# Attention with a gated MLP on one core: the score shift split on another engine, another order at the start and at the end

## The chip, the cores and the metric

The kernel runs on one core of a Trainium2 chip. A core has five engines that run their own queues side by side: TensorE (PE) multiplies matrices, VectorE (DVE) and ScalarE (ACT) work elementwise and can read the accumulator memory (PSUM), GpSimd (POOL) works elementwise on the on-chip memory (SBUF) alone, and SyncE (SP) issues the transfers between SBUF and device memory. Each queue is worked off in order, and engines wait for each other by semaphores. The metric is the device time of one execution in microseconds (us), as the median of several runs.

## What is computed

The sequence has 2048 tokens of 512 numbers, with 32 heads of 16 and 1792 hidden columns in the MLP. All inputs are fp32.

```python
xn = layernorm(x)                               # eps 1e-5, no scale or offset
q, k, v = split(xn @ wqkv)                      # 32 heads of 16
p = softmax(q @ k.T * 16 ** -0.5)               # 2048 x 2048 in each head
s = concat(p @ v) @ wo
h = relu(xn @ w1 + b1) ** 2
g = silu(h @ w2 + b2)
out = x + s * g
```

## The kernel before

**Split numbers.** A product of fp32 accuracy is made of three faster ones. A tensor is split into a high part (rounded to fp32r, the format of the faster product) and a low part (what the rounding left), and `a @ b` becomes high x high, high x low and low x high, summed in PSUM. The helper `split` (line 95) makes both parts on GpSimd: a `tensor_scalar` (times 1, plus 0) for the high part, a `tensor_tensor` subtraction for the low one.

**The head.** Sixteen token tiles of 128 rows are loaded, normalized, transposed on TensorE and split. `ln_stats` takes mean and variance on VectorE and the square root on ScalarE; `ln_norm` makes the two scalars of each token on VectorE and the normalized tile on ScalarE (line 1236); `ln_high` transposes it on TensorE (four products with the identity) and copies the high part out of PSUM on ScalarE; `ln_low` takes the low part on VectorE. `split_w` splits the weights of the first q and k columns, high part on ScalarE, low part on GpSimd. The loop at line 1322 hands these out for tile after tile, and `pump(n)` puts n products of q, k or v in between. The order of PE's queue there is that of the program. The first products belong to the k columns (m = 4) of the first 256 tokens, thus to tiles 0 and 1; `qk_terms` puts them in an order by the parts that they need.

**The lead and the loop.** A unit is one group of four heads and 512 queries; there are 32. For each, 64 products of raw scores (64x512, line 320) are made ahead, each reduced to its maximum per row on VectorE (line 327). `shift(u)` turns the maxima of unit u by a 32x32 transpose (`tr`), negates and splits them into `sh` with two VectorE instructions (lines 373 and 376), and SyncE stores `sh` in device memory (`keep`) and loads it back as two more rows of the q tile (`back`, four transfers). The K tile has rows of 1.0 at the same place (`fill_ring("ka", ...)`), so that the second product of the scores (line 1281) comes out with the maximum taken off; ScalarE takes its exponential (line 1293), and line 408 multiplies it with v. The code counts by slots: in each the two halves of PE's rows work on different products, among them the MLP and later the output product, and in a slot eight PV products (line 408, four heads by one block of keys) stand together. In the first chunk of the MLP GpSimd also splits w1 and w2, which it later reads back from device memory or keeps. In the loop, the order on ScalarE, VectorE, GpSimd and SyncE is that of the program.

**The end.** `unit_final` closes the last unit for the last four token tiles: twelve products add the last heads to four sums in PSUM (`out(tt, n)`; n = 2 needs the low part that GpSimd makes), `gate` multiplies each by g on VectorE, tile 1 gets its residual sum by a product with the identity and a ScalarE copy, and `add` adds it for tiles 0 and 2 on GpSimd and for tile 3 on VectorE. Four stores end the kernel.

Of the kernel before, what the change touches and what calls it, by code (L numbers as in the profile page):

```python
# [9 lines left out]
F32 = mybir.dt.float32  # L10
F32R = mybir.dt.float32r
AF = mybir.ActivationFunctionType
ALU = mybir.AluOpType
# [4 lines left out]
P = 128  # L18
# [7 lines left out]
NT = S // P  # L26
NQ = H // 4
NU = NQ * 4
# [29 lines left out]
def kernel(  # L58
# [11 lines left out]
    nc = tc.nc  # L70
# [44 lines left out]
    with ExitStack() as ph:  # L115
# [253 lines left out]
        def shift(u):  # L369
            tr = sp.tile([P, 32], F32, name="tr", bufs=1)  # L370
            nc.vector.transpose(tr, mxs[u])
            sh = sp.tile([P, 2, 32], F32R, name="sh", bufs=1)
            nc.vector.scalar_tensor_tensor(
                sh[:, 0], tr, -2.0, tr, op0=ALU.mult, op1=ALU.add
            )
            nc.vector.scalar_tensor_tensor(
                sh[:, 1], tr, -1.0, sh[:, 0].bitcast(F32),
                op0=ALU.mult, op1=ALU.subtract,
            )

            def keep():
                nc.sync.dma_start(
                    sh_d[u].rearrange("b c i n -> (b c) i n"), sh.bitcast(F32)
                )
# [536 lines left out]
        def unit_final(po):  # L921
# [24 lines left out]
                g = parts[tt][0]  # L946
                nc.vector.tensor_tensor(g, pss[tt], g, op=ALU.mult)

            def add(tt, eng):
                g, s = parts[tt]  # L950
                eng.tensor_tensor(g, g, s, op=ALU.add)

            def store(tt, queue):
                queue.dma_start(of[1536 + tt * P : 1536 + (tt + 1) * P, :], parts[tt][0])

            for i in range(2):
                for tt, n in ((0, 0), (0, 1), (1, 0), (1, 1), (0, 2), (1, 2)):
                    out(2 * i + tt, n)
            for tt in range(4):
                gate(tt)  # L960
            nc.tensor.matmul(both, ident, parts[1][0], start=False, stop=True)
            nc.scalar.activation(parts[1][0], both, AF.Copy)
            add(0, nc.gpsimd)
            add(2, nc.gpsimd)
            add(3, nc.vector)
            store(0, nc.sync)
            store(1, nc.scalar)
            store(2, nc.scalar)
            store(3, nc.sync)

        ph.enter_context(tc.manual_schedule(engines={mybir.EngineType.PE}))
        qs = ExitStack()
# [57 lines left out]


# [179 lines left out]
        xts = {}  # L1211
# [17 lines left out]
        def ln_norm(t):  # L1229
            rstd = rstds.pop(t)  # L1230
            xn = xp.tile([P, D], F32, name="xn", bufs=3)
            nc.vector.reciprocal(rstd[:, 0:1], rstd[:, 0:1])
            nc.vector.tensor_scalar(
                rstd[:, 1:2], mvs.pop(t)[:, 0:1], rstd[:, 0:1], -1.0, op0=ALU.mult, op1=ALU.mult
            )
            nc.scalar.activation(xn, xts[t], AF.Identity, bias=rstd[:, 1:2], scale=rstd[:, 0:1])
            xts[t] = xn

        def ln_high(t):
# [78 lines left out]
            load_x(t)  # L1318
        for vt in vts:
            nc.vector.memset(vt[:, :, DH:], 1.0)  # L1320
        fill_ring("ka", 0, 1.0)
        for i in range(NT + 3):
            if i in (2, 3):

                kos = slice(2 * i - 4, 2 * i - 2)
                if i == 2:
                    ln_norm(1)
                    ln_high(0)
                    split_w(wa_t, kos, slice(0, 2 * P), raw_m[:, kos])
                else:  # L1330
                    ln_low(0)
                    ln_high(1)
                    split_w(wa_t, kos, slice(0, 2 * P), raw_m[:, kos])
                    ln_norm(2)
                ln_stats(i)
            else:
                if i < NT:
                    ln_stats(i)
                if 0 <= i - 1 < NT:
                    ln_norm(i - 1)  # L1340
                if 0 <= i - 3 < NT:
                    ln_low(i - 3)
                if i == 4:

                    pump(4)
                if 0 <= i - 2 < NT:
                    ln_high(i - 2)
            if 5 <= i < 9:
                split_w(wa_t, i - 5, slice(2 * P, 2 * P + D), raw_v[:, i - 5], True)
            let_go()  # L1350
            if 9 <= i < 11:
                fill_ring("ka", 1, 1.0, (32 + 64 * (i - 9),))
            if i in (11, 12):
                fill_ring("qm", i - 11, 0.0)
            if i == 11:
# [40 lines left out]
        fill_ring("qm", 2, 0.0)  # L1396
        for n in range(4):
            fill_ring("qe", n, 0.0)
        fill_ring("ka", 2, 1.0)
        pump(47)  # L1400
        led.append(0)
        at = order.index(("v", 2, 0)) + 1
# [323 lines left out]
```

## Time and profile before

| | |
|---|---|
| median of 3 runs | 1624.79 us (1623.78 to 1625.50) |
| the profiled execution | 1623.51 us, its span 1621.7 us |
| PE busy | 1608.4 us (99%) |
| VectorE busy | 1362.7 us (84%) |
| ScalarE busy | 1189.5 us (73%) |
| GpSimd busy | 520.7 us (32%) |
| 16 DMA engines, mean of packets' time in the main queue | 44.3% of the span |
| VectorE: maxima from PSUM (line 327, main group) | 1910 x 682 ns |
| VectorE: transposes of the shift (line 371) | 32 x 200 ns |

A row of the timeline reads: start (us from the span's start), duration, engine, line, operation, written tile, read tiles, shapes, count of merged instructions, and in brackets the idle time ahead and what ended it. A row of the windows view gives the stretch, its length, the busy time and count of PE, PE's weight loads, VectorE, ScalarE and GpSimd, then the granted clock of TensorE, the share of the DMA engines and GB/s. The chain of waits goes back from the last instruction to what released each step.

### The profile page before, as it was taken

The numbers are of one execution on the slowest core, as the hardware profiler recorded it, in microseconds if no ns is written. First come the engines' busy times: TensorE is split into PE (matmuls) and PEld (weight loads), VectorE is DVE, ScalarE is ACT, GpSimd is POOL, SyncE is SP. The second block draws the span as 40 slices with busy tenths as digits, with TensorE's granted clock in tenths as the row PEclk, the third lists the DMA queues.
The fourth block names the chain that finished last, engine by engine and source line by source line (L and its number), as shares of the span: only waits on it lengthen the run. The fifth ranks groups of instructions, "written<-read, shape, count | busy, mean of one in ns | idle before, by whom it ended". The sixth has DMA issues, their size and how long they took to land.

```text
span 1621.7 us, 36039 instructions
## 1 busy us (share of the span) xinstructions
PE 1608.4 (99%) x13660; PEld 933.3 (58%) x13660; DVE 1362.7 (84%) x2364; ACT 1189.5 (73%) x2349; POOL 520.7 (32%) x550
## 2 busy tenths in 40 slices
PE   8999999999999999999999999999999999999998
PEld 6898665556546654664466446645654565445543
DVE  6486888888888888888888888888888888887755
ACT  7212677777777777877777777777777777778886
POOL 6436667133113311331132113311331123214621
PEclk9999999999999999999999999999999999999999
DMA  8876556434342333423333334323432262236654
GB/s 295 239 237 230 175 165 154 132 94 130 79 105 89 110 84 91 132 87 101 91 108 99 88 92 118 113 73 90 131 109 71 65 162 76 65 106 219 213 176 169
DMA packets 164028, 209.18 MB, mean 129 GB/s; under 512 B 59120, under 2 KB 79088, under 8 KB 162288
## 3 DMA queue, kind: packets, MB, share of 16 engines
q1 hardware_dynamic: 163568, 206.37, 44.3%
q8 instruction: 108, 1.77, 0.5%
q14 instruction: 64, 0.52, 0.1%
q10 hardware_dynamic: 288, 0.52, 0.1%
HBM read 148.90 MB, written 56.34 MB: 127 GB/s over the span
## 4 chain that ended last, share of the span: by engine, by line
PE 98%; DVE 1%; DMA 0%; SPq 0%; issue 0%; DVEq 0%
PE po L408 31%; PE pd_t L258 19%; PE pm_t L320 17%; PE se L1281 15%; PE pd_t L226 5%; PE pm_t L1157 4%; PE pm_t L226 2%; PE pd_t L1157 1%; PE se L1127 1%; PE se L1061 1%; PE se L320 1%; DVE mx L327 0%; PE pm_t L1243 0%; PE pd_t L1127 0%; DMA xt<-in_A_x_dram 0%; PE po L1061 0%
## 5 line engine op out<-in xcount | busy, mean ns | idle before, releaser
L327 DVE TENSOR_REDUCE mx<-pm_t 128x1 f32<-128x512 f32 x1910 | 1187.0, 682 | 163.1 <-PE pm_t L320 80.2
L1293 ACT ACTIVATE pt<-se 128x512 f32<-128x512 f32 x1894 | 976.1, 613 | 235.0 <-PE se L1281 192.5
L320 PE MATMUL pm_t<-ka,qm 64*128 64x512 f32 x1910 | 761.7, 419 | 0.1
L1281 PE MATMUL se<-qe,ka 64*128 64x512 f32 x2005 | 677.6, 396 | 0.0
L408 PE MATMUL po<-pt,v 128*32 128x512 f32 x3820 | 520.8, 605 | 0.2 <-DVE tsm L851 0.2
L320 PEld LDWEIGHTS pm_t<-ka,qm 64*128 64x128 f32 x1910 | 335.1, 184 | 236.5 <-DVE mx L327 225.5
L1281 PEld LDWEIGHTS se<-qe,ka 64*128 64x128 f32 x2005 | 339.1, 184 | 19.7 <-ACT xr L1293 1.7
L258 PEld LDWEIGHTS pd_t<-xc,w1s 64*128 64x128 f32 x2352 | 292.0, 186 | 82.2 <-issue 82.2
L258 PE MATMUL pd_t<-xc,w1s 64*128 64x256 f32 x2352 | 332.2, 288 | 0.0
L258 PE MATMUL pd_t<-w2t,hT 64*128 64x512 f32 x1080 | 300.5, 410 | 0.0
L258 PEld LDWEIGHTS pd_t<-w2t,hT 64*128 64x128 f32 x1080 | 179.1, 184 | 82.3 <-issue 75.5
L573 POOL TENSOR_TENSOR r<-r 128x512 f32<-128x512 f32 x56 | 58.2, 1040 | 370.5 <-ACT r L570 370.5
L408 PEld LDWEIGHTS po<-pt,v 128*32 128x32 f32 x3820 | 76.7, 108 | 147.2 <-issue 125.8
L592 POOL TENSOR_TENSOR u<-u,b_t 128x512 f32<-128x512 f32 x16 | 20.6, 1288 | 317.7 <-ACT u L591 283.9
L327 DVE TENSOR_REDUCE mx<-se 128x1 f32<-128x512 f32 x121 | 77.9, 685 | 26.1 <-PE se L320 21.6
L457 POOL TENSOR_TENSOR ot<-ot,hl 128x512 f32<-128x512 f32 x27 | 34.7, 1286 | 168.5 <-DMA hl<-r_d 101.6
L570 ACT ACTIVATE r<-pd_t,b_t 128x256 f32<-128x256 f32 x112 | 46.9, 470 | 57.0 <-PE pd_t L258 55.9
L1157 PE MATMUL pm_t<-xT,wr_t 64*128 64x512 f32 x408 | 73.8, 388 | 0.0
L100 POOL TENSOR_TENSOR hT<-r,hT 128x512 fp32r<-128x512 f32 x56 | 72.2, 1290 | 4.7
L226 PE MATMUL pd_t<-w2t,hT 64*128 64x512 f32 x264 | 68.9, 393 | 0.0
L1157 PEld LDWEIGHTS pm_t<-xT,wr_t 64*128 64x128 f32 x408 | 58.2, 185 | 4.4
L226 PEld LDWEIGHTS pd_t<-w2t,hT 64*128 64x128 f32 x264 | 47.1, 184 | 6.4 <-issue 0.2
(174 smaller groups left out, 1352.2 us busy)
## 6 DMA issues: line engine op xcount, KB each, us to landing
w1s<-w_d SPq DMA_DIRECT2D x196, 256.0 KB
qm<-q_d SPq DMA_DIRECT2D x384, 32.0 KB
ka<-k_d SPq DMA_DIRECT2D x96, 128.0 KB
qe<-q_d SPq DMA_DIRECT2D x384, 32.0 KB
q_d<-hl SPq DMA_DIRECT2D x16, 512.0 KB
g<-g_d SPq DMA_DIRECT2D x32, 256.0 KB
k_d<-hl SPq DMA_DIRECT2D x15, 512.0 KB
on_d<-hl SPq DMA_DIRECT2D x116, 64.0 KB
```

The costliest lines, as they stand in the source:

```text
L100: (lo or nc.gpsimd).tensor_tensor(dst[1], raw, dst[0].bitcast(F32), op=ALU.subtract)
L226: mm = nc.tensor.matmul(out_, lh(r), rh(r), start=first_ and lane == 0, stop=last_ and lane == 1, skip_group_check=True,)
L258: mm = nc.tensor.matmul(out_, lh(r), rh(r), start=first_ and lane == 0, stop=last_ and lane == 1, skip_group_check=True,)
L320: nc.tensor.matmul(ps, qms[u][p][64 * j : 64 * j + 64, qb * P : (qb + 1) * P], kas[qd, p][64 * j : 64 * j + 64, kc * 512 : (kc + 1) * 512] ...
L327: return nc.vector.tensor_reduce(mxs[u][:, c, kc : kc + 1], ps, axis=AX.X, op=ALU.max)
L408: nc.tensor.matmul(po[32 * j : 32 * j + 32, :], vs[qd][:, (4 * kb + j) * VW : (4 * kb + j) * VW + 32], pts[j], start=(kb == 0), stop=(kb = ...
L457: nc.gpsimd.tensor_tensor(ot, ot, rb, op=ALU.mult)
L570: nc.scalar.activation(r[:, i], ps[:, i * CW : (i + 1) * CW], AF.Relu, bias=b1_t[:, fo : fo + 1])
L573: nc.gpsimd.tensor_tensor(r, r, r, op=ALU.mult)
L1157: mm = nc.tensor.matmul(out_, lh(r), rh(r), start=first_ and lane == first, stop=last_ and lane != first, skip_group_check=True,)
L1281: nc.tensor.matmul(se, kas[qd, j // 2][b : b + 64, kb * P : (kb + 1) * P], qes[u][j // 2][b : b + 64, :], start=True, stop=True,)
L1293: return nc.scalar.activation(pts[j], se, AF.Exp, scale=0.25)
```

## The change

1. The shift. For units 1 to 30 the two parts are made by `split` on GpSimd instead of VectorE. Units 0 and 31 keep VectorE, with a `tensor_scalar` and a `tensor_tensor`. The maxima are no longer negated, and the rows in K are -1 instead of 1.
2. The head. Tiles 0 and 1 are normalized by VectorE. Their low parts are taken directly behind their transposes in the program, tile 2's statistics after tile 0's low part. Ten products (before: four) stand ahead of tile 2's transposes; the first twelve come in another order (all high x high first, those with the low part of the weights' second half last). The counts of later pumps change so that their sum stays.
3. The end. The third product of token tiles 0 and 2 comes one place earlier; the sum of tile 2 is made by halves of 256 columns, one on GpSimd and one on VectorE; tile 2 is stored in halves, and all stores but tile 1's go through SyncE.

```diff
-            nc.vector.scalar_tensor_tensor(
-                sh[:, 0], tr, -2.0, tr, op0=ALU.mult, op1=ALU.add
-            )
-            nc.vector.scalar_tensor_tensor(
-                sh[:, 1], tr, -1.0, sh[:, 0].bitcast(F32),
-                op0=ALU.mult, op1=ALU.subtract,
-            )
+            if u in (0, NU - 1):
+                nc.vector.tensor_scalar(sh[:, 0], tr, 1.0, None, op0=ALU.mult)
+                nc.vector.tensor_tensor(sh[:, 1], tr, sh[:, 0].bitcast(F32), op=ALU.subtract)
+            else:
+                split((sh[:, 0], sh[:, 1]), tr)
...
-            def add(tt, eng):
+            def add(tt, eng, cols=slice(0, 512)):
                 g, s = parts[tt]
-                eng.tensor_tensor(g, g, s, op=ALU.add)
+                eng.tensor_tensor(g[:, cols], g[:, cols], s[:, cols], op=ALU.add)
...
-                for tt, n in ((0, 0), (0, 1), (1, 0), (1, 1), (0, 2), (1, 2)):
+                for tt, n in ((0, 0), (0, 1), (1, 0), (0, 2), (1, 1), (1, 2)):
...
             add(0, nc.gpsimd)
-            add(2, nc.gpsimd)
+            add(2, nc.gpsimd, slice(0, 256))
             add(3, nc.vector)
+            add(2, nc.vector, slice(256, 512))
             store(0, nc.sync)
             store(1, nc.scalar)
-            store(2, nc.scalar)
+            store(2, nc.sync, slice(0, 256))
             store(3, nc.sync)
+            store(2, nc.sync, slice(256, 512))
...
-                t = [t[k] for k in (0, 2, 3, 5, 1, 4)] + t[6:]
+                t = [t[k] for k in (0, 3, 6, 9, 2, 5, 1, 4, 7, 10, 8, 11)]
...
-            nc.scalar.activation(xn, xts[t], AF.Identity, bias=rstd[:, 1:2], scale=rstd[:, 0:1])
+            if t < 2:
+                nc.vector.tensor_scalar(
+                    xn, xts[t], rstd[:, 0:1], rstd[:, 1:2], op0=ALU.mult, op1=ALU.add
+                )
+            else:
+                nc.scalar.activation(xn, xts[t], AF.Identity, bias=rstd[:, 1:2], scale=rstd[:, 0:1])
...
-        fill_ring("ka", 0, 1.0)
+        fill_ring("ka", 0, -1.0)
...
                     split_w(wa_t, kos, slice(0, 2 * P), raw_m[:, kos])
+                    ln_low(0)
                 else:
-                    ln_low(0)
                     ln_high(1)
                     split_w(wa_t, kos, slice(0, 2 * P), raw_m[:, kos])
+                    ln_stats(2)
+                    ln_low(1)
                     ln_norm(2)
-                ln_stats(i)
+                    ln_stats(3)
...
-                if 0 <= i - 3 < NT:
+                if 2 <= i - 3 < NT:
                     ln_low(i - 3)
                 if i == 4:
-                    pump(4)
+                    pump(10)
...
-                pump({4: 4, 7: 14, 8: 12}.get(i, 8 if i < 7 else 7))
+                pump({4: 6, 7: 14, 8: 12}.get(i, 8 if i < 7 else 7 if i < 11 else 6))
```

PE's queue at the start of the program, before (L1243 are the transposes of the token tiles, four per tile; L1061 the products of the k and q columns, from the split tiles xT and weights wa_t):

```order
L1243 MATMUL pm_t<-ident,xn 128x128 x8
L1061 MATMUL se<-xT_192,wa_t 128x256 x4
L1243 MATMUL pm_t<-ident,xn 128x128 x4
L1061 MATMUL se<-xT_192,wa_t 128x256 x4
L1243 MATMUL pm_t<-ident,xn 128x128 x4
L1061 MATMUL se<-xT_192,wa_t 128x256 x8
```

and with the change (the transposes are now L1248):

```order
L1248 MATMUL pm_t<-ident,xn 128x128 x8
L1061 MATMUL se<-xT_192,wa_t 128x256 x10
L1248 MATMUL pm_t<-ident,xn 128x128 x4
L1061 MATMUL se<-xT_192,wa_t 128x256 x6
L1248 MATMUL pm_t<-ident,xn 128x128 x4
L1061 MATMUL se<-xT_192,wa_t 128x256 x8
```

Six more products stand ahead of tile 2's transposes (the second L1243 row), eight more ahead of tile 3's.

VectorE's queue at the same place, before (statistics L1223 and L1225, the scalars L1232 and L1233, the low part L1251), from tile 0's scalars on:

```order
L1232 RECIPROCAL rstd<-rstd 128x1
L1233 TENSOR_SCALAR rstd<-mv,rstd 128x1
L1232 RECIPROCAL rstd<-rstd 128x1
L1233 TENSOR_SCALAR rstd<-mv,rstd 128x1
L1223 BN_STATS stats<-xt 128x6
L1225 BN_AGGR mv<-stats 128x2
L1251 TENSOR_TENSOR xT_192<-pm_t,xT_192 128x4x128
```

and with the change (the normalization is L1237, the low part L1256):

```order
L1232 RECIPROCAL rstd<-rstd 128x1
L1233 TENSOR_SCALAR rstd<-mv,rstd 128x1
L1237 TENSOR_SCALAR xn<-xt,rstd 128x512
L1232 RECIPROCAL rstd<-rstd 128x1
L1233 TENSOR_SCALAR rstd<-mv,rstd 128x1
L1237 TENSOR_SCALAR xn<-xt,rstd 128x512
L1256 TENSOR_TENSOR xT_192<-pm_t,xT_192 128x4x128
L1223 BN_STATS stats<-xt 128x6
L1225 BN_AGGR mv<-stats 128x2
L1256 TENSOR_TENSOR xT_192<-pm_t,xT_192 128x4x128
```

The two normalizations stand between the scalars, and both low parts now come before tile 2's scalars; the statistics of tile 2 moved behind the first of them.

GpSimd's queue in the loop with the change, at the shift of unit 2 in the MLP's first chunk (w1s and w2t are the split weights, ex their raw loads, r the squared hidden tile):

```order
L99 TENSOR_SCALAR w1s_1510<-ex_1502 128x256
L100 TENSOR_TENSOR w1s_1510<-ex_1502,w1s_1510 128x256
L99 TENSOR_SCALAR sh<-tr 128x32
L100 TENSOR_TENSOR sh<-tr,sh 128x32
L99 TENSOR_SCALAR w2t<-ex_1501 128x512
L100 TENSOR_TENSOR w2t<-ex_1501,w2t 128x512
L571 TENSOR_TENSOR r_2404<-r_2404 128x512
```

The two `sh` rows are new; before, the w1 split was followed at once by that of w2, and the shift's two instructions stood in VectorE's queue behind the transpose.

More of the change, by code (lines that the diff above doesn't have):

```diff
@@ L947, in gate, with store @@
                 nc.vector.tensor_tensor(g, pss[tt], g, op=ALU.mult)
-            def add(tt, eng):
+            def add(tt, eng, cols=slice(0, 512)):
                 g, s = parts[tt]
-                eng.tensor_tensor(g, g, s, op=ALU.add)
-            def store(tt, queue):
-                queue.dma_start(of[1536 + tt * P : 1536 + (tt + 1) * P, :], parts[tt][0])
+                eng.tensor_tensor(g[:, cols], g[:, cols], s[:, cols], op=ALU.add)
+            def store(tt, queue, cols=slice(0, 512)):
+                queue.dma_start(of[1536 + tt * P : 1536 + (tt + 1) * P, cols], parts[tt][0][:, cols])
             for i in range(2):
-                for tt, n in ((0, 0), (0, 1), (1, 0), (1, 1), (0, 2), (1, 2)):
+                for tt, n in ((0, 0), (0, 1), (1, 0), (0, 2), (1, 1), (1, 2)):
                     out(2 * i + tt, n)
@@ L1351 @@
             if 9 <= i < 11:
-                fill_ring("ka", 1, 1.0, (32 + 64 * (i - 9),))
+                fill_ring("ka", 1, -1.0, (32 + 64 * (i - 9),))
             if i in (11, 12):
@@ L1398 @@
             fill_ring("qe", n, 0.0)
-        fill_ring("ka", 2, 1.0)
+        fill_ring("ka", 2, -1.0)
         pump(47)
```

## The prediction

> **What bounds the kernel now.** I read the page first (the span and the chain of waits), then one long window of the middle, then single slots around a shift, and last the two ends.
>
> The span and the chain's shares by engine, from the page, and the busy time of each engine from 300 to 1450 us:
>
> ```profile
> span 1621.7 us, 36039 instructions
> PE 98%; DVE 1%; DMA 0%; SPq 0%; issue 0%; DVEq 0%
> 300.00:1450.00 1150.00, 1150.00 (x10071) 635.13 (x10064) 1022.78 (x1742) 889.00 (x1768) 275.92 (x274) 1.00 0.36 98
> ```
>
> TensorE (PE) is the chain. In the middle it is busy for 1150.00 of 1150 us at a granted clock of 1.00; VectorE (DVE, third figure) is at 89%, GpSimd (POOL, fifth) at 24%. Matmul ends are modelled, so the row alone doesn't prove that PE never waits. The test is a slot with a shift in it: does PE's rhythm slip? VectorE around the shift of unit 8, and the first of each slot's eight PV products on PE at the same time:
>
> ```profile
> 508.97 0.20 DVE L371 STREAM_TRANSPOSE tr<-m 128x32 f32<-128x32 f32 x1
> 509.20 0.19 DVE L373 SCALAR_TENSOR_TENSOR sh<-tr 128x32 fp32r<-128x32 f32 x1
> 509.43 0.19 DVE L376 SCALAR_TENSOR_TENSOR sh<-tr,sh 128x32 fp32r<-128x32 f32 x1
> 509.58 1.89 DVE L327 TENSOR_REDUCE mx<-pm_t 128x1 f32<-128x512 f32 x3
> 511.67 3.08 DVE L327 TENSOR_REDUCE mx<-pm_t 128x1 f32<-128x512 f32 x5 [0.20 <-PE pm_t L320]
> ```
>
> ```profile
> 508.01 1.07 PE L408 MATMUL po<-pt,v 128*32 128x512 f32 x8
> 510.13 1.06 PE L408 MATMUL po<-pt,v 128*32 128x512 f32 x8
> 513.71 1.07 PE L408 MATMUL po<-pt,v 128*32 128x512 f32 x8
> 519.42 1.06 PE L408 MATMUL po<-pt,v 128*32 128x512 f32 x8
> ```
>
> The pair of slots with the shift takes 513.71 - 508.01 = 5.70 us, the next pair without one 5.71. The three shift instructions cost VectorE about 0.6 us, and three reductions later it waits for PE again (0.20 us). So an ordinary shift is absorbed, and VectorE time taken out of it buys nothing.
>
> **The shift split, part by part.** All splits on VectorE, then the two that stand out, with what GpSimd did then and what PE did:
>
> ```profile
> L373 DVE SCALAR_TENSOR_TENSOR sh<-tr x32: 191/193/994, 119.0 to 1555.3; 128x32 fp32r<-128x32 f32 x32
> ```
>
> ```profile
> 234.14 0.98 DVE L373 SCALAR_TENSOR_TENSOR sh<-tr 128x32 fp32r<-128x32 f32 x1
> 1374.28 0.99 DVE L373 SCALAR_TENSOR_TENSOR sh<-tr 128x32 fp32r<-128x32 f32 x1
> ```
>
> ```profile
> 233.78 1.29 POOL L100 TENSOR_TENSOR w2t<-ex,w2t 128x512 fp32r<-128x512 f32 x1
> 1373.94 1.29 POOL L100 TENSOR_TENSOR wot<-wraw,wot 128x512 fp32r<-128x512 f32 x1
> ```
>
> ```profile
> 235.07 1.06 PE L408 MATMUL po<-pt,v 128*32 128x512 f32 x8
> 239.20 1.07 PE L408 MATMUL po<-pt,v 128*32 128x512 f32 x8
> 1375.18 1.06 PE L408 MATMUL po<-pt,v 128*32 128x512 f32 x8
> 1379.21 1.07 PE L408 MATMUL po<-pt,v 128*32 128x512 f32 x8
> ```
>
> The median split takes 0.193 us, two take five times that, and both end as a GpSimd subtraction of 128x512 ends: 234.14 + 0.98 = 235.12 against 233.78 + 1.29 = 235.07; 1374.28 + 0.99 = 1375.27 against 1373.94 + 1.29 = 1375.23. VectorE stands still while GpSimd works, and this time PE notices: its next gap is 4.13 us (235.07 to 239.20) and 4.03 us (1375.18 to 1379.21), where the same half of a pair takes 513.71 - 510.13 = 3.58. The first costs 0.55, the second 0.45. Units 2 and 27 are among the 30 that move, so **1.0 us** comes off. The other 28 give 0. Bounds: 0.45, if unit 2 loses its share as below, to 1.1.
>
> On the other side, GpSimd now has two instructions of 128x32 per unit, and SyncE's queue store of the shift waits for them. At 27 of the 30 units GpSimd, busy for 24% of the loop, is through with what stands ahead before the transpose ends (compared unit by unit in the timeline), so they start at once. At units 1 and 2 they stand behind the splits of w1, at unit 30 behind that of the last output weights. The end of the w1 splits and the store at unit 2, and the store at unit 30 behind its split:
>
> ```profile
> 239.09 0.73 POOL L100 TENSOR_TENSOR w1s<-ex,w1s 128x256 fp32r<-128x256 f32 x1
> 237.90 0.38 SPq L382 DMA_DIRECT2D sh_d<-sh  x1
> 1510.29 0.19 DVE L376 SCALAR_TENSOR_TENSOR sh<-tr,sh 128x32 fp32r<-128x32 f32 x1
> 1514.14 0.42 SPq L382 DMA_DIRECT2D sh_d<-sh  x1
> ```
>
> The price of a 128x32 pair on GpSimd isn't in the trace: not over 0.73 each (the 128x256 subtraction), not under nothing; by that row's columns I take 0.25 each. At unit 2 the store moves from 237.90 to about 239.82 + 0.5 = 240.3, 2.4 us later, and SyncE's queue behind it (the reciprocals' way back, loads of w2, the four row loads of the shift) with it. At unit 30 the store already goes out 3.7 us after the split's end and PE shows no wait for the rows, so 2.4 us more at unit 2 is likely slack. I take 0. The K rows of -1 are the same memsets with another number, and units 0 and 31 keep two small VectorE instructions: 0.
>
> **The head.** The scalars of tile 0, the two normalizations on ScalarE (ACT), tile 2's statistics behind a DMA, ScalarE's copy that the first product waits for, then PE, the first maxima, and PE's settled rate in the chain:
>
> ```profile
> 5.39 0.21 DVE L1233 TENSOR_SCALAR rstd<-mv,rstd 128x1 f32<-128x1 f32 x1
> 5.64 1.52 ACT L1236 ACTIVATE xn<-xt,rstd 128x512 f32<-128x512 f32 x2
> 7.86 0.69 DVE L1223 BATCH_NORM_STATS2 stats<-xt 128x6 f32<-128x512 f32 x1 [1.77 <-DMA xt<-in_A_x_dram]
> 9.00 0.58 ACT L1245 ACTIVATE xT<-pm_t 128x512 fp32r<-128x512 f32 x1
> 6.60 1.94 PE L1243 MATMUL pm_t<-ident,xn 128*128 128x128 f32 x8 [6.60 <-ACT xn L1236]
> 9.63 1.68 PE L1061 MATMUL se<-xT,wa_t 128*128 128x256 f32 x4 [1.09 <-ACT xT L1245]
> 11.10 1.05 PE L1243 MATMUL pm_t<-ident,xn 128*128 128x128 f32 x4
> 12.22 1.23 PE L1061 MATMUL se<-xT,wa_t 128*128 128x256 f32 x4
> 64.59 7.33 DVE L327 TENSOR_REDUCE mx<-se 128x1 f32<-128x512 f32 x12 [2.36 <-PE se L320]
> ```
>
> ```profile
> 19.41 1.18 PE se L1061 x10
> ```
>
> *Normalization on VectorE.* No row has a wide tensor_scalar on VectorE: it costs between 0.21 (128x1) and 0.69 (the statistics, which read the same 512 columns). I take 0.69. Tile 0 is then ready at 5.63 + 0.69 = 6.32 instead of about 6.4, and, with tile 1's scalars (0.3) between, tile 1 at 7.3 against 7.16. Transposes start 0.1 us earlier. ScalarE, free of 1.52 us and no longer taking tile 2's square root between its two copies, ends the second copy near 9.15 instead of 9.58: the first product starts at about 9.2 instead of 9.63.
>
> *Ten products first.* Before, four products and tile 2's transposes stood ahead of 12.22, where PE waited for VectorE's low part of tile 1. Ten products at 1.23/4 = 0.31 run from 9.2 to 12.3, the seventh (11.05) needing that low part, which comes at about 8.3 + 0.6 + 0.7 + 0.2 + 0.7 = 10.5 (low part of tile 0, statistics, aggregate, low part of tile 1). So at 12.3 ten products are done, where it was four and transposes worth 1.05/0.31 = 3.4 more. That is 2.6 x 0.31 = **0.8 us**. From there to the first maxima at 64.59, which wait for PE and not for their loads, nothing else is in the chain, so the lead stays. Lower bound: if PE's early slow rate ends at the same time after launch anyway, the 2.6 products count at 1.18/10 = 0.12: 0.3. Upper: 0.21-us normalizations bring the first product 0.45 us sooner, 1.25; and if the slow rate ends another microsecond sooner after a start without gaps, that is worth 1 - 0.12/0.31 = 0.6 more: 1.8.
>
> [...] The granted-clock column says 1.00 from the start, but 0.31 against 0.12 us per product agrees with a slow start.
>
> **The end.** The last two gates and adds on VectorE, GpSimd's low part and its second add:
>
> ```profile
> 1614.24 0.74 POOL L934 TENSOR_TENSOR thl<-tot,thl 128x256 fp32r<-128x256 f32 x1 [0.82 <-ACT thl L933]
> 1615.67 0.69 DVE L947 TENSOR_TENSOR g<-pm_t,g 128x512 f32<-128x512 f32 x1 [0.24 <-PE pm_t L940]
> 1616.28 0.68 DVE L947 TENSOR_TENSOR g<-pd_t,g 128x512 f32<-128x512 f32 x1
> 1616.44 1.26 POOL L951 TENSOR_TENSOR g<-g,ts 128x512 f32<-128x512 f32 x1 [0.22 <-DVE g L947]
> 1616.99 1.26 DVE L951 TENSOR_TENSOR g<-g,ts 128x512 f32<-128x512 f32 x1
> ```
>
> Token tile 2's last product goes one place earlier, so its gate starts up to 0.24 us earlier, and so does the next: the last add starts near 1616.77. Before, it took 1.26 us, until 0.55 us after GpSimd's add (1617.70). Now GpSimd adds half of tile 2, 0.74 by its 128x256 row: from 1616.2 (its low part ends at 1614.98, its first add takes 1.26) to 1617.0. VectorE's add then ends near 1617.5, its half of tile 2 costs half of 0.69, some 0.4 with the start, and the last store is free at 1617.9 instead of 1618.25: **0.4 us**. Bounds: 0 (the smaller store lands no sooner) to 0.7.
>
> **The sum.** 1.0 + 0.8 + 0.4 = 2.2 us. The profiled execution took 1623.51, so it would become 1621.3; it lies 1.3 below the median of the runs (1624.79), and against that the forecast is 1622.6.
>
> **Rivals.**
> *VectorE bounds the whole loop* and each unit gives back the 0.38 us of two splits: 30 x 0.38 = 11.4, so 1624.79 - 11.4 - 1.2 = 1612.2. For it: 89% busy. Against: the 5.70 and 5.71 us above, equal with and without a shift.
> *The head's gain is given back*: VectorE, with 2 x 0.69 us more in its queue, delivers later tiles late, or the first maxima wait for their DMAs at 64 us. Then 1.0 + 0.4 remain: 1623.4. Against: each later tile's transposes now stand behind six to eight more products (0.7 to 0.9 us), which gives VectorE that much.
> *GpSimd's queue at unit 2* (and, shorter, at unit 1): the split waits there from the transpose (234.1) to the end of the w1 splits (239.82), 5.7 us; SyncE stands behind it, and PE waits for w2 or shift rows. If all of that reached PE, and unit 2's 0.55 were lost: 1624.79 + 5.7 - 1.65 = 1628.8. It decides once the rows come later than the 3.7 us that unit 30 already bears.
> *More of everything*: 1.1 + 1.8 + 0.7 = 3.6, 1621.2.
>
> **How the numbers follow.** Forecast case 0.50 (its own range 1621.2 to 1624.0, from 3.6 and 0.75 us of gain), near its upper end or beyond 0.18, the head given back 0.14, GpSimd's queue 0.10, VectorE the bound 0.08. A change under 0.2% (3.25 us) can't be told from none here. Faster by more: 0.08 of VectorE, 0.15 of the 0.18 and 0.04 of the forecast case, 0.27. Slower by more: 0.07 of GpSimd's queue and 0.04 for prices that no row names, 0.11. The rest, 0.62, is within. The range runs from 1620.0, past all the gains, to 1625.5, where GpSimd's queue costs 2.4 us.
>
> **What would show it.** Right: no split on VectorE but two; PV gaps of 3.5 to 3.6 us at units 2 and 27; the first product near 9.2 us and the first maxima some 0.8 us before 64.59; a last VectorE add of under 0.8 us. Wrong: PV gaps shorter than 5.70 per pair all through the loop (VectorE was the bound), PE waits for GpSimd or DMA between 190 and 300 us, or the lead of the head gone by 64 us.

## The result and the profile after

The changed kernel takes 1621.18 us (median of 19 runs, 1620.79 to 1621.7), the kernel before, on the same chip, 1624.27 (19 runs, 1623.4 to 1625.5). The ratio is 0.9981, 95% interval 0.9974 to 0.9988: 3.1 us less, 1.9 to 4.2. The forecast was 1622.6 with a range of 1620.0 to 1625.5. The profiled execution took 1621.38 us, 2.1 less than the profiled execution of before (1623.51); the difference of 1.0 between the two figures is a finding below.

The head of the page of the changed kernel, and its chain of waits by engine:

```profile
span 1619.6 us, 36065 instructions
PE 99%; DVE 1%; DMA 0%; issue 0%; ACT 0%; DVEq 0%
```

TensorE is still the chain, so the way to compare is by TensorE's own milestones. The first of the eight PV products of every slot (510 groups in each trace) were set side by side; "lead" is by how much one comes sooner than in the profiled execution of before. The lead is 0.65 us at the first (170.63 before, 169.98 after), rises by 0.55 at unit 2 and by 0.5 at unit 27, and stands at 2.1 us at the last (1607.53 and 1605.41); most of the 0.4 that these three don't explain appears near 1571 us (see the first experiment). From the last PV product to the end of the span it is 14.1 us before and 14.2 after. So the head and the two shifts paid, the end did not.

The head of the changed kernel on TensorE, with the start of the first maxima on VectorE, and then two groups of transposes in the kernel before:

```profile
6.24 1.94 PE L1248 MATMUL pm_t<-ident,xn 128*128 128x128 f32 x8 [6.24 <-DVE rstd L1232]
9.02 2.60 PE L1061 MATMUL se<-xT,wa_t 128*128 128x256 f32 x10 [0.84 <-ACT xT L1250]
11.41 1.05 PE L1248 MATMUL pm_t<-ident,xn 128*128 128x128 f32 x4
13.54 1.05 PE L1248 MATMUL pm_t<-ident,xn 128*128 128x128 f32 x4
15.56 0.60 PE L1248 MATMUL pm_t<-ident,xn 128*128 128x128 f32 x4
```

```profile
63.90 2.55 DVE L327 TENSOR_REDUCE mx<-se 128x1 f32<-128x512 f32 x4 [2.36 <-PE se L320]
```

```profile
13.24 1.05 PE L1243 MATMUL pm_t<-ident,xn 128*128 128x128 f32 x4
15.32 0.60 PE L1243 MATMUL pm_t<-ident,xn 128*128 128x128 f32 x4
```

Ten products run in 11.41 - 9.02 = 2.39 us, 0.24 each. The transposes show TensorE's slow start: four take 1.05 us at 13.54 and 0.60 at 15.56, so the fast rate begins between them. Before, this switch lay between 13.24 and 15.32. By the starts of the single matmuls, which are 0.21 us apart at the slow rate and 0.11 to 0.12 at the fast one, it came at about 14.9 us with the change and at 14.7 before, nearly the same time. The first maxima come at 63.90 instead of 64.59, 0.69 sooner.

The shift split in the groups by tile (shortest, median and longest in ns), and the PV products at units 2 and 27:

```profile
L99 POOL TENSOR_SCALAR sh<-tr x30: 209/217/219, 191.5 to 1509.9; 128x32 fp32r<-128x32 f32 x30
L100 POOL TENSOR_TENSOR sh<-tr,sh x30: 250/253/258, 191.8 to 1510.2; 128x32 fp32r<-128x32 f32 x30
L374 DVE TENSOR_SCALAR sh<-tr x2: 182/301/420, 118.5 to 1553.6; 128x32 fp32r<-128x32 f32 x2
```

```profile
234.44 1.07 PE L406 MATMUL po<-pt,v 128*32 128x512 f32 x8
238.00 1.07 PE L406 MATMUL po<-pt,v 128*32 128x512 f32 x8
1373.91 1.06 PE L406 MATMUL po<-pt,v 128*32 128x512 f32 x8
1377.44 1.06 PE L406 MATMUL po<-pt,v 128*32 128x512 f32 x8
```

The gaps are 3.56 and 3.53 us, where they were 4.13 and 4.03.

The end: the two adds that VectorE makes last (0.72 and 0.41 us, merged in the row), and then four of the stretches of 0.4 us in which the last stores travel (the last two figures are the busy share of the DMA engines and GB/s):

```profile
1614.78 1.05 DVE L949 TENSOR_TENSOR g<-g,ts 128x512 f32<-128x512 f32 x2
```

```profile
1616.00:1616.40 0.40, 0.00 (x0) 0.00 (x0) 0.00 (x0) 0.00 (x0) 0.00 (x0) 1.00 0.78 241
1616.40:1616.80 0.40, 0.00 (x0) 0.00 (x0) 0.00 (x0) 0.00 (x0) 0.00 (x0) 1.00 1.04 389
1617.60:1618.00 0.40, 0.00 (x0) 0.00 (x0) 0.00 (x0) 0.00 (x0) 0.00 (x0) 1.00 1.02 348
1618.00:1618.40 0.40, 0.00 (x0) 0.00 (x0) 0.00 (x0) 0.00 (x0) 0.00 (x0) 1.00 0.33 108
```

The last add ends at 1615.83, 10.4 us after the last PV product, where it was 10.7. But the DMA engines are then full until about 1618.2, and that sets the end, as the run with one store less shows.

### The profile page after: what moved, and what is told of

It is laid out like the page before. It is cut to its first block, busy times and chain, and to the rows that moved or that the text cites. A ratio compares the mean times of both kernels' runs of the same rounds, so it can differ in the third digit from the quotient of the medians.

```text
span 1619.6 us, 36065 instructions
## 1 busy us (share of the span) xinstructions
PE 1607.3 (99%) x13660; PEld 939.7 (58%) x13660; DVE 1352.4 (84%) x2307; ACT 1187.2 (73%) x2347; POOL 534.1 (33%) x610
## 4 chain that ended last, share of the span: by engine, by line
PE 99%; DVE 1%; DMA 0%; issue 0%; ACT 0%; DVEq 0%
PE po L406 31%; PE pd_t L258 19%; PE pm_t L320 17%; PE se L1286 15%; PE pd_t L226 5%; PE pm_t L1157 4%; PE pm_t L226 1%; PE pd_t L1157 1%; PE se L1127 1%; PE se L1061 1%; PE se L320 1%; PE pm_t L1248 0%; PE pd_t L1127 0%; DVE mx L327 0%; PE po L1061 0%; DMA xt<-in_A_x_dram 0%
## 5 line engine op out<-in xcount | busy, mean ns | idle before, releaser
L258 PEld LDWEIGHTS pd_t<-w2t,hT 64*128 64x128 f32 x1080 | 179.3, 184 | 82.4 <-issue 75.5
L99 POOL TENSOR_SCALAR sh<-tr 128x32 fp32r<-128x32 f32 x30 | 6.5, 217 | 213.6 <-DVE tr L371 213.6
```

The lines of the kernel that those rows point to most:

```text
L258: mm = nc.tensor.matmul(out_, lh(r), rh(r), start=first_ and lane == 0, stop=last_ and lane == 1, skip_group_check=True,)
```

## The experiments

Times are medians of 11 runs beside runs of the kernel before: 33 of them (1624.42) for the shift, the two units, the whole head and the end, 20 (1624.12) for the normalizations alone and the first run with added products, 21 (1624.9) for the order alone and the second run with added products. The kernels without a store and with delays are single runs.

**The shift part alone.**

```diff
-            nc.vector.scalar_tensor_tensor(
...
+            if u in (0, NU - 1):
+                nc.vector.tensor_scalar(sh[:, 0], tr, 1.0, None, op0=ALU.mult)
+                nc.vector.tensor_tensor(sh[:, 1], tr, sh[:, 0].bitcast(F32), op=ALU.subtract)
+            else:
+                split((sh[:, 0], sh[:, 1]), tr)
...
-        fill_ring("ka", 0, 1.0)
+        fill_ring("ka", 0, -1.0)
```

> The kernel before with the shift part alone (the split on GpSimd for units 1 to 30, two small VectorE instructions for units 0 and 31, K rows of -1). Theory (only the two stalls at units 2 and 27 count): the PV products start as before up to unit 2, 0.5 to 0.6 us sooner from there, 1.0 to 1.1 us sooner from unit 27 on, and nothing else in the loop moves; time 1.1 us under that of before. Rival (VectorE's time counts in every unit): a lead that grows by 0.38 us per unit, 11 us in all. Rival (GpSimd's queue costs PE at units 1, 2 or 30): the lead shrinks there by 1 us or more. Open: a further 0.3 us that the changed kernel gained near 1571 us, at the end of the loop; if it belongs to the shift it appears here too, and the sum is 1.4.

1622.71 us, ratio 0.9991 (0.9982 to 1.0), 1.7 us less. The PV products at the two units:

```profile
235.95 1.07 PE L406 MATMUL po<-pt,v 128*32 128x512 f32 x8
239.51 1.07 PE L406 MATMUL po<-pt,v 128*32 128x512 f32 x8
1375.42 1.06 PE L406 MATMUL po<-pt,v 128*32 128x512 f32 x8
1378.94 1.07 PE L406 MATMUL po<-pt,v 128*32 128x512 f32 x8
```

Gaps of 3.56 and 3.52 again; the lead rises by 0.56 and by 0.58 there and nowhere by 0.38 a unit, so VectorE does not bound the loop. Two things were not expected. This run began behind: its first PV product is at 171.50 us, 0.9 later than before, though nothing ahead of it had changed. And the further gain near 1571 us appears in every run, of whatever part (0.2 to 0.3 us, in the run with the end alone too): the one profiled execution of before was slow there, and it is no effect of the change.

**The shift on GpSimd in two units** (the edit is against the run above).

```diff
-            if u in (0, NU - 1):
+            if u not in (2, 27):
```

> The kernel before with K rows of -1, but the shift split on GpSimd for units 2 and 27 alone; the other 30 units keep two small instructions on VectorE (a copy and a subtraction). Theory: all of the shift part's gain is in these two units, so 1.0 to 1.1 us under before, 0.5 to 0.6 at unit 2 and 0.5 at unit 27, as in the run with the whole part; a rest that the whole part gains near 1571 us and this one doesn't belongs to unit 31's or unit 30's shift. Rival (the other 28 units count too): clearly less than the whole part gains.

1622.79 us, ratio 0.9991 (0.9982 to 1.0), as much as the whole part: +0.57 at unit 2, +0.56 at unit 27, nothing that the whole part has and this one lacks. The other 28 units give nothing in these executions.

**The head alone** (the diff's lines from the term order down, without the K rows).

```diff
-                t = [t[k] for k in (0, 2, 3, 5, 1, 4)] + t[6:]
+                t = [t[k] for k in (0, 3, 6, 9, 2, 5, 1, 4, 7, 10, 8, 11)]
...
+            if t < 2:
+                nc.vector.tensor_scalar(
...
-                    pump(4)
+                    pump(10)
```

> The kernel before with the head part alone (two normalizations on VectorE, order of statistics and low parts, ten products ahead). Theory: the first maxima start 0.7 us before 64.59, the PV products are 0.65 us sooner from the first (171.25 us before) to the last, nothing is added or lost in between, time 0.7 us under before. Rival (the lead is given back): under 0.2 us at the first PV product or at the end.

1622.64 us, ratio 0.9988 (0.9979 to 0.9997), 1.8 us less, more than the 0.7 expected. The lead is 1.19 at the first PV product: the switch to the fast rate came at 13.6 us here, 1.3 us sooner than in the changed kernel with the same head. And 0.5 of it is lost at unit 3. VectorE's first shift instruction there, and what GpSimd did:

```profile
285.02 0.76 DVE L373 SCALAR_TENSOR_TENSOR sh<-tr 128x32 fp32r<-128x32 f32 x1
284.45 1.28 POOL L457 TENSOR_TENSOR ot<-ot,hl 128x512 f32<-128x512 f32 x1 [1.90 <-DMA hl<-r_d]
```

It is the stall of units 2 and 27 at a third unit: VectorE's instruction ends (285.78) as GpSimd's does (285.73). In the profiled execution of before the two had passed each other by 0.05 us, 286.41 + 0.19 = 286.60 against 286.65:

```profile
286.41 0.19 DVE L376 SCALAR_TENSOR_TENSOR sh<-tr,sh 128x32 fp32r<-128x32 f32 x1
286.65 1.29 POOL L457 TENSOR_TENSOR ot<-ot,hl 128x512 f32<-128x512 f32 x1 [2.26 <-DMA hl<-r_d]
```

GpSimd's start there hangs on a DMA (1.90 and 2.26 us of waiting in the two rows), VectorE's on TensorE (the maxima ahead of it wait 0.40 us for it), so which comes first can differ from run to run. The two places of the prediction did not vary: in all five profiled executions with the old shift (before, the head, the normalizations, the order and the end alone) VectorE's first instruction took 0.98 to 1.01 us at units 2 and 27.

**The normalizations on VectorE alone** (only the second hunk of the diff above).

> The kernel before with the two normalizations of the first tiles on VectorE and nothing else. Theory (in the head only PE work done before PE's switch to its fast rate counts, and that switch comes at 13.5 to 15.9 us, different from run to run): first product at 9.0 to 9.2 us instead of 9.5 to 10.0, but the fifth product still waits for the low part of tile 1, so the second four start within 0.3 us of before (12.2); time 0 to 0.3 us under before. Rival (the normalization is the gain, the ten products are not): 0.5 to 0.7 us under.

1623.71 us, ratio 0.9997 (0.9988 to 1.0006). The step to 9.0 failed: the first product is at 9.69. ScalarE and TensorE there:

```profile
8.85 0.29 ACT L1227 ACTIVATE rstd<-mv,eps_t 128x1 f32<-128x1 f32 x1 [0.30 <-DVE mv L1225]
9.05 0.58 ACT L1250 ACTIVATE xT<-pm_t 128x512 fp32r<-128x512 f32 x1
9.69 1.35 PE L1061 MATMUL se<-xT,wa_t 128*128 128x256 f32 x4 [1.43 <-ACT xT L1250]
```

ScalarE has no normalization to make any more, but tile 2's square root still stands ahead of its second copy. The lead at the first PV product is 0.05 us. At unit 3 this run loses 0.9: its second shift instruction on VectorE takes 1.20 us.

**The head's order alone**, with the normalizations on ScalarE (the edit is against the run with the head alone).

```diff
-            if t < 2:
+            if t < 0:
```

> The kernel before with the head part except for the normalizations, which stay on ScalarE: order of statistics and low parts, ten products ahead. Theory (the unbroken start is the gain, and with it PE's fast rate comes sooner): first product at 9.3 to 9.7 us, then no PE wait before the third tile's transposes; PV products 0.5 to 1.2 us sooner than in the kernel before, time 0.5 to 1.2 us under; together with the 0.4 us that the normalizations alone gave, within 0.5 of the 1.5 us of the whole head part. Rival (the normalizations must be on VectorE for the ten products to fit): a PE wait of over 0.5 us before the fifth to seventh product, and under 0.3 us of gain.

1623.77 us beside 1624.9 of before (21 runs), ratio 0.9991 (0.9982 to 1.0). First product at 9.32, no long wait of TensorE after it, and the first maxima at 63.75, 0.84 sooner than before, where they are at 64.39 with the normalizations alone. In both of these runs the switch came at about 14.2 us, so with an equal switch, one execution each, the order is ahead of the normalizations by 0.6 us and carries most of the head; the normalizations add 0.3 at the first product (9.02 against 9.32). The lead is down to 0.43 at the first PV product, for a reason that was not looked for, and then 1.1 is lost at unit 3 (a shift instruction of 1.30 us).

**The end alone.**

```diff
-                for tt, n in ((0, 0), (0, 1), (1, 0), (1, 1), (0, 2), (1, 2)):
+                for tt, n in ((0, 0), (0, 1), (1, 0), (0, 2), (1, 1), (1, 2)):
...
-            add(2, nc.gpsimd)
+            add(2, nc.gpsimd, slice(0, 256))
             add(3, nc.vector)
+            add(2, nc.vector, slice(256, 512))
...
```

> The kernel before with the end part alone (token tile 2's last product one place sooner, its sum in two halves, three of the four stores of the last 512 rows on SyncE). Theory A (the last add sets the end): the last VectorE add ends 0.3 to 0.4 us sooner after the last PV product, and the span ends as much sooner: 13.7 us from the last PV product to the end, where it was 14.1. Theory B (the last stores are limited by what the DMA engines move): the add ends sooner, but 14.1 us stay from the last PV product to the end; time as before within 0.1 us.

1623.8 us, ratio 0.9994 (0.9986 to 1.0003), which alone decides nothing. By the trace it is 14.15 us from the last PV product (1607.65) to the end of the span (1621.8), as before, though the last add ends 10.4 us after that product, 0.3 sooner: theory B.

**One store less.** The store of token tile 1 is left out, so 128 rows of the output are not written.

```diff
-            store(1, nc.scalar)
```

> The changed kernel without the store of the last unit's token tile 1 (256 KB of the output are not written); its sum is still made. That store is neither the first nor the last of the five. Theory (the last stores are limited by what the DMA engines move, 385 GB/s): 0.3 to 0.7 us less from the last PV product to the end, 13.5 to 13.9 instead of 14.2. Rival (the last add, its issue and a fixed landing time set the end): 14.2 as before.

The last add ends 10.4 us after the last PV product (1605.22), as in the changed kernel, and the last bytes travel at about 1617.3:

```profile
1616.40:1616.80 0.40, 0.00 (x0) 0.00 (x0) 0.00 (x0) 0.00 (x0) 0.00 (x0) 1.00 1.05 394
1616.80:1617.20 0.40, 0.00 (x0) 0.00 (x0) 0.00 (x0) 0.00 (x0) 0.00 (x0) 1.00 0.96 325
1617.20:1617.60 0.40, 0.00 (x0) 0.00 (x0) 0.00 (x0) 0.00 (x0) 0.00 (x0) 1.00 0.22 69
```

The end comes 13.5 us after the last PV product instead of 14.2: 0.7 less, and 256 KB at 385 GB/s are 0.68 us. A store that is neither first nor last shortens the end by its bytes (in one execution), so the bytes set it.

**TensorE kept at work from 3.2 us.** To the changed kernel, products that nobody reads are added, to see whether the fast rate comes sooner by TensorE's work.

```diff
+        hot = pe.tile([P, 512], F32, name="se")
+        for _ in range(11):
+            nc.tensor.matmul(hot[:, :P], ident, ident, start=True, stop=True)
...
+                    for _ in range(3):
+                        nc.tensor.matmul(hot[:, :P], ident, ident, start=True, stop=True)
```

> The changed kernel with 14 products of the identity with itself added on TensorE, whose result nobody reads: 11 from 3.2 us, when the identity is there, to the first transposes, and 3 in the 0.84 us in which PE waits for ScalarE's copies. [...] Rival (the switch has its time after launch, whatever PE does): switch at 13.5 to 15.9, first maxima and time as in the changed kernel within 0.5 us. Rival (an early fast rate is useless, since the tiles come no sooner): switch early, PE waits before the transposes of tiles 2 to 6, and less than 0.5 us of it is left at the first PV product.

1622.73 us, ratio 0.9992 to before (0.9983 to 1.0001), slower than the changed kernel. TensorE in it:

```profile
3.23 5.06 PE L1329 MATMUL se<-ident 128*128 128x128 f32 x22 [3.23 <-POOL ident masks.py:199]
8.08 1.21 PE L1248 MATMUL pm_t<-ident,xn 128*128 128x128 f32 x8
10.54 1.91 PE L1061 MATMUL se<-xT,wa_t 128*128 128x256 f32 x10 [0.59 <-ACT xT L1250]
12.83 0.66 PE L1248 MATMUL pm_t<-ident,xn 128*128 128x128 f32 x4 [0.37 <-ACT xn L1241]
```

Each of the eleven added products shows as two matmuls, 22 in 4.85 us, so they last until about 8.1 and hold the transposes up by 1.8. But the eight transposes then take 1.21 us, where they took 1.94: by their single starts the fast rate is there at about 8.4, where no execution without added products has it before 12.9. In this run, then, the switch follows from TensorE's work and not from the time after launch. It is of little use, for at 12.83 TensorE waits for ScalarE's normalization.

**The same with 6 and 1 products**, and at the end token tile 0's sum and store in halves.

```diff
+            add(0, nc.gpsimd, slice(0, 256))
+            add(0, nc.gpsimd, slice(256, 512))
...
+            store(0, nc.sync, slice(0, 256))
+            store(0, nc.scalar, slice(256, 512))
```

> The changed kernel with 6 idle products of the identity from 3.2 us and 1 before the first product (the first try with 14 of them took 0.46 us each and held the transposes up by 1.8 us), and at the end with token tile 0's sum and store in two halves, so that the first bytes leave sooner; the second half goes out on ScalarE's queue. Head, theory (unbroken work brings the fast rate; it came at 8.2 us in the first try): transposes from 6.2 to 6.4 as in the changed kernel, switch before 10 us, PE then waits for tiles 2 and 3, so 0.3 to 1.0 us of it is left at the first PV product (169.0 to 169.7, where the changed kernel had 169.98). Head, rival: switch at 13 to 15, first PV product between 169.4 and 170.0 as without them. End, theory (bytes limit it): 13.6 to 13.9 us from the last PV product to the end instead of 14.2; rival (the last add and its issue limit it): 14.2. Time 1620 to 1621.

1621.44 us, ratio 0.998 to before (0.9971 to 0.9988): no better than the changed kernel (0.9981). In the head:

```profile
7.95 0.64 PE L1344 MATMUL se<-ident 128*128 128x128 f32 x2
8.95 2.59 PE L1063 MATMUL se<-xT,wa_t 128*128 128x256 f32 x10 [0.36 <-ACT xT L1252]
11.34 1.05 PE L1250 MATMUL pm_t<-ident,xn 128*128 128x128 f32 x4
13.14 0.66 PE L1250 MATMUL pm_t<-ident,xn 128*128 128x128 f32 x4
```

5.4 us of work from 3.2 to 8.6, with one pause of 0.2 us near 6, did not bring the fast rate, and after the pause of 0.36 us it came at about 12.6, so the expected switch before 10 us failed. The first PV product is at 169.84, within the rival's range. The end took 14.4 us instead of 14.2: the second half's store waits on ScalarE's queue behind the copy of tile 1, nothing travels from 1615.2 to 1615.6, and the bytes come in one run after that all the same.

**GpSimd delayed ahead of the shift split.** Copies of tr into a tile that nobody reads stand ahead of the split: 10, 20, 30, 40 and 60 at units 6, 10, 14, 18 and 22.

```diff
             else:
+                for _ in range({6: 10, 10: 20, 14: 30, 18: 40, 22: 60}.get(u, 0)):
+                    zz = sp.tile([P, 32], F32, name="zz", bufs=1)
+                    nc.gpsimd.tensor_scalar(zz, tr, 1.0, 0.0, op0=ALU.mult, op1=ALU.add)
                 split((sh[:, 0], sh[:, 1]), tr)
```

> The changed kernel with 10, 20, 30, 40 and 60 added GpSimd instructions of 128x32, 0.22 us each, ahead of the shift split of units 6, 10, 14, 18 and 22: the split comes 2.2, 4.4, 6.6, 8.8 and 13 us later. Theory (the shift rows have slack of more than 4 us, which is why unit 2's late store cost nothing): no PE wait at units 6 and 10; from some delay between 4.4 and 13 us on, a PE wait that grows by as much as the delay grows. Rival (GpSimd's queue decides from 3.7 us on): 0.7 us lost at unit 10, 2.9 at 14, 5.1 at 18, 9 at 22.

From start to start such an instruction takes 0.30 us, not 0.22, so the delays were 2.9, 5.9, 8.9, 11.9 and 17.9 us. Against the changed kernel the PV products lost 0 at unit 6, 0.9 at unit 10, 0 at unit 14, 1.7 at unit 18 and 8.9 at unit 22, where the waits of TensorE from 300 to 1200 us (total, times, longest) show, with 5.9 of the 8.9, a load of w1 that stood behind the shift's store in SyncE's queue:

```profile
PE pd_t L258 <- DMA w1s<-w_d: 6.3, 2, 5.9
```

So the queue does reach TensorE, but its price is not the delay less a fixed slack: it hangs on what stands behind.

**5.9 us at every third unit** (20 such copies at units 2, 5 and so on to 29; meant as 4.4). In the first run TensorE was granted a clock of 0.85 throughout (span 1740.6 us), which says nothing of the delays; the kernel ran again.

> The changed kernel with 20 added GpSimd instructions of 128x32 (4.4 us) ahead of the shift split of units 2, 5, 8 and so on to 29, ten in all. In the run with five delays 2.2 us cost nothing, 4.4 cost 1.0 us at unit 10 (by way of ScalarE, which waited for GpSimd), 6.6 nothing at unit 14, 8.8 1.7 us at unit 18, 13 us 8.9 at unit 22. Theory (slack of 4 us and more in most units, unit 2 among them): at most 1.2 us lost at any unit and 0 to 4 us in all. Rival of the prediction (at unit 2 PE loses whatever comes on top of 3.7 us): unit 2, where the split already stands 5.7 us, loses 4 us.

> The same kernel with ten delays of 4.4 us once more, since TensorE was granted a clock of 0.85 throughout the first run. Theory (slack of 4 us and more in most units, unit 2 among them): at most 1.2 us lost at any unit and 0 to 4 us in all against the changed kernel. Rival of the prediction (at unit 2 PE loses whatever comes on top of 3.7 us): unit 2, where the split already stands 5.7 us, loses 4 us.

1631.3 us. Against the changed kernel unit 2 lost 5.8 us, units 5, 8, 11 and 14 nothing, unit 17 0.9, units 20 to 26 nothing, units 29 and 30 together 3.5. My theory fell at unit 2, where even the rival had 4 us. The waits of TensorE between 200 and 300 us (total, times, longest) with GpSimd's split of the piece of w2 that they wait for, and then, in the changed kernel, the split of the same piece and TensorE's use of it there:

```profile
PE pd_t L226 <- POOL w2t L99: 1.6, 1, 1.6
PE pd_t L226 <- POOL w2t L100: 0.9, 1, 0.9
```

```profile
272.70 1.27 POOL L100 TENSOR_TENSOR w2t<-ex,w2t 128x512 fp32r<-128x512 f32 x1
```

```profile
267.33 1.28 POOL L100 TENSOR_TENSOR w2t<-ex,w2t 128x512 fp32r<-128x512 f32 x1
271.40 0.39 PE L226 MATMUL pd_t<-w2t,hT 64*128 64x512 f32 x1
```

What TensorE waits for at unit 2 is not the shift's rows, but the splits of w2, which stand on GpSimd behind the shift and whose loads stand behind it in SyncE's queue. In the changed kernel the low part of the piece is ready at 268.61 and used from about 271.6 on: 3.0 us of slack. The delay of 5.9 brings the piece 5.4 us later, at 273.97, which exceeds the slack by 2.4; the two waits are 2.5 together. The lead falls by more, in two steps of 3.5 and 2.3 us; that the rest comes from the following pieces, loaded one after the other, is likely but not shown.

## Why the prediction was right, and where it was not

**The shift, 1.0 us: right in mechanism, a little small, and not the whole of it.** Units 2 and 27 gave 0.55 and 0.5 in the changed kernel, 0.56 and 0.57 in the runs that tried them apart, so 1.1, the upper bound. "The other 28 give 0" held for the profiled execution and not in general: unit 3 was 0.05 us from the same stall, and in all three runs with a new head and the old shift (the head, the normalizations and the order alone) it cost 0.5 to 1.1 us. Moving the shift to GpSimd removed that too. How many of the plain runs of before have the stall at unit 3 was not measured; the second profiled execution with the old head and the old shift (the end alone) passed it as well, by 0.07 us.

**The shift's price, 0: right, with less room than was thought.** The pair on GpSimd takes 0.22 and 0.25 us (0.25 each was taken, though the columns of the row quoted for it give only 0.09). The queue store at unit 2 now:

```profile
239.74 0.32 SPq L380 DMA_DIRECT2D sh_d<-sh  x1
```

It was at 237.90; with TensorE 0.65 ahead by then that is 2.5 us later against it, where 2.4 was forecast, and TensorE did not wait. The rival of GpSimd's queue named the right place, and of its two victims, w2 and the shift's rows, it is w2: some 3 us more there would have reached TensorE.

**The head, 0.8 us: near in number, by other terms, and so in part by luck.** By the one pair of profiles it is 0.65 at the first PV product. Of the sub-steps, the normalization took 0.55 us (0.69 taken), the first product came at 9.02 (9.2), and products at the slow rate start 0.21 us apart, not 0.31, since the 1.23 us of the group of four run past the next matmul's start (12.22 + 1.23 = 13.45 against 13.24) and its first step is 0.38. The step that missed is the "2.6 x 0.31". In this pair the switch came at nearly the same time, 14.7 and 14.9 us, which is the case of the lower bound: a matmul done ahead of it saves only the 0.12 us that it would take at the fast rate. But seven more were done by then, not 2.6 (19 before and 26 after, behind the first eight transposes): 7 x 0.12, less some 0.1 for the later switch, is 0.7.

The pair is not the whole of it either. Over the executions with the new head and nothing else ahead of the first PV product (169.98, 169.44, 169.78, 169.59, 169.53) and those with the old (170.63, 171.50, 170.92, 171.12) it is 171.04 - 169.66 = 1.4, and no new one is as late as any old one. In these the switch came at 12.9 to 14.9 us with the new head and at 14.7 to 16.3 with the old, 1.5 us sooner on the average, and a microsecond of that is worth about 1 - 0.12/0.21 = 0.4 us (the head alone against the changed kernel: 1.3 us sooner, and the first PV product 0.54). So what was held for the upper bound counts too, with about 0.6 beside the 0.8 of the seven matmuls: gapless work that starts sooner switches sooner, not in every pair but on the average of these executions. That the switch has a fixed time after launch is refuted by the one run that has it at 8.4 us, with TensorE busy from 3.23.

From the start of gapless work to the switch it took 5.2 us in the first run with added products (3.23 to about 8.4), 3.6 in the second (8.95 to about 12.6) and 3.7 to 5.9 from the first product with the new head. Why the 5.4 us of work from 3.2 to 8.6 in the second run did not bring it, with one pause of 0.2 us, no run shows.

**The end, 0.4 us: wrong; its lower bound came.** The add ended 0.3 us sooner, as forecast, and the step from there to the end of the span failed: the last three stores share the DMA engines at some 385 GB/s, and their 640 KB take 1.7 us, which an add that ends 0.3 us sooner does not shorten. The rows for that were in the trace of before, where the last add ends at 1618.25 and 768 KB follow:

```profile
1618.40:1618.80 0.40, 0.00 (x0) 0.00 (x0) 0.00 (x0) 0.00 (x0) 0.00 (x0) 1.00 1.05 389
1620.00:1620.40 0.40, 0.00 (x0) 0.00 (x0) 0.00 (x0) 0.00 (x0) 0.00 (x0) 0.50 0.85 318
```

The prediction looked only at engines there.

**The sum.** The forecast of 1622.6 counted from 1624.79; beside the change the kernel before measured 1624.27. 1.1 + 1.4 + 0 = 2.5, and up to 1.1 more where unit 3 stalls: 2.5 to 3.6 against 3.1 measured (1.9 to 4.2). The difference of 1.0 between the two figures of the result is for the most part the head's spread: the profiled execution of before has the earliest first PV product of the four with the old head, 0.4 ahead of their mean, and that of the changed kernel the latest of its five, 0.3 behind theirs. So 2.2 was too low by a head that varies, and the error at the end hid part of it; whether the stall at unit 3 makes up the rest is open. Of the rivals, VectorE as the bound is refuted (no lead grows along the loop), the head given back too (its lead reaches the end), and "more of everything" came closest in its number, 1621.2, but not by its terms: the end gave nothing.

## What to carry to other kernels

A stall that shows in two of thirty places is a sample of a collision: look how far the others are from it, and count a move that takes the cause away a little above what one profile shows. Before shortening the last computation ahead of the last stores, ask whether the DMA engines are already full there (a busy share of 1.0 at some 385 GB/s here); if so, fewer bytes help (256 KB less were worth 0.7 us here), and whether earlier bytes would, no run here shows. A head that one profile dates is dated to within half a microsecond to one, because TensorE's switch to its fast rate moves from run to run (12.9 to 16.3 us here without added products); compare several executions by the first product that both kernels have in common.

## What the runs showed of the hardware

VectorE stood still in instructions with one input as well as with two. At unit 31 of the changed kernel the copy with one input took 0.42 us, where it took 0.18 at unit 0; from VectorE's and GpSimd's timeline:

```profile
1553.58 0.42 DVE L374 TENSOR_SCALAR sh<-tr 128x32 fp32r<-128x32 f32 x1
1552.68 1.28 POOL L793 TENSOR_TENSOR ts<-ts,xr 128x512 f32<-128x512 f32 x1
```

It ends at 1554.00, GpSimd's addition at 1553.96. In five other places it was the same: units 2 and 27 before, and unit 3 with the head, the normalizations and the order alone. Each time a VectorE instruction of 128x32 began during a GpSimd `tensor_tensor` of 128x512 (1.28 to 1.30 us) and ended 0.04 to 0.05 us after it: up to 1.3 us went into one that takes 0.19 (unit 3 with the head's order alone). What makes VectorE wait, no run shows.

The column of granted clock reads 1.00 in the stretches from 8 to 15 us, before and with the change, while four transposes take 1.05 us before the switch and 0.60 after it: the slow start is visible in durations only.
